# Attention scores: another order of sixteen key tiles, with one exponential over two neighbouring PSUM banks for ten of 32 score pairs

## The chip, the core and the metric

The kernel runs on one core of a Trainium2 chip. Its time is device microseconds of one execution. PE is the matrix engine (PEld is its weight loads), DVE the vector engine, ACT the scalar engine, POOL GpSimd, SP the engine that starts the DMAs.

## The reference, cut to what matters

Two layers, each an attention block and an MLP, on 2048 rows of 640 values in float32. The change touches attention alone:

```python
qkv = (x @ wqkv).reshape(B, S, 3, H, Dh)          # S 2048, H 32 heads, Dh 20
scores = einsum("bhqd,bhkd->bhqk", q, k) * Dh ** -0.5
p = softmax(scores, axis=-1)
o = einsum("bhqk,bhkd->bhqd", p, v)               # then @ wo, added to x
x = x + attention(layernorm(x)); x = x + mlp(layernorm(x))      # twice
```

## The kernel before

After the projections, attention runs in 32 blocks a layer. A block is four heads (a group g) and 512 queries (qb); it walks over sixteen tiles of 128 keys (kt). For each key tile there are four score matmuls (`score`, L713), one a head, each 128 keys by 512 queries into one PSUM bank; an exponential of each by ACT into an SBUF tile (L720), which is the softmax numerator because the row maximum is already subtracted through two extra rows of q and k; and the PV step (`pv`, L725), which adds exp times v of the four heads into bank 7. A 21st column of v gives the sum of the exponentials.

The four heads of a group are two pairs p, and of each pair one head (par 0) lies on PE's rows 0 to 63, the other (par 1) on rows 64 to 127, so that matmuls of different par run side by side.

The row maxima of a block have to be there before its scores. They are computed two blocks ahead, among the scores of the present block: a matmul with queries on the partitions (`by_queries`, L619) into a bank, and a maximum over it by DVE (L630). When all maxima of a block are there, `mrows_max` and `mrows` reduce and transpose them (two small DVE operations, L674 and L685), POOL splits them into two parts and a DMA writes them out; `mrows_load` brings them back two key tiles later as rows of q. This is called behind a PV step: at the first one at which the maxima are complete and the scores have begun key tile 4 of the block two ahead of the use (`state["begun"] >= (t - 2) * NKT + 4`). At the end of a block `finish` copies bank 7 (DVE, L738); its division follows in six steps in the next block, by POOL and DMAs.

What is issued when is written out by hand, in one string for the sixteen key tiles of a block (`ORDER_OF_BLOCK`, L1028), which `op` reads letter by letter (L1092): a and b are the next score of par 0 and of par 1 with its exponential, m and n the next maximum of par 0 and par 1, and V the next PV step. Each engine runs its instructions in the order in which they are issued. Four scores (abab) are issued ahead of the first block. When the maxima have run out, m and n do nothing. DMAs of q, k and v are started by `begin`, the first time that a score of a key tile is issued.

Seven banks (0 to 6) serve scores and maxima. Which one a row takes is decided while the kernel is built, by `Clock` (L505), a small model of PE, ACT and DVE in ns: it books each row's start, the exponential's or maximum's end and from that when each bank is free, and gives the bank that is free first. `value` books the PV step and the DVE operations that come with it: the copy at the last key tile, and 340 ns at key tile 4 for the two small ones. The model sets no order and adds no wait, it only chooses banks; semaphores keep the order between engines on the chip.

Of the kernel before, what the change touches and what calls it, by code (L numbers as in the profile page):

```python
# [10 lines left out]
AF = mybir.ActivationFunctionType  # L11
# [6 lines left out]
S = 2048  # L18
# [9 lines left out]
NKT = S // P  # L28
# [4 lines left out]
SCALE = DH ** -0.5  # L33
# [6 lines left out]
def tile_layers(  # L40
# [11 lines left out]
    nc = tc.nc  # L52
# [28 lines left out]
    banks = psum.tile([P, 8, 512], F32, tag="banks", name="banks")  # L81
# [424 lines left out]
    class Clock:  # L506
# [6 lines left out]
            self.act, self.act_end, self.dve = 0, 0, 0  # L513
            self.ready, self.used, self.acc = {}, [], 0

        def row(self, par):
            b = min(range(7), key=self.free.__getitem__)
            s = self.now + 3
            if self.values:
                s = self.now + 542  # L520
                self.values, self.fresh, self.place = False, [True, True], 0
                self.lane, self.over, self.since = [0, 0], [0, 0], None
            s = max(s, self.lane[par], self.load)
            w = max(s - 116, self.free[b] + 34)
            t = max(s, w + 61)
            more = max(0, w + 116 - t)
            if self.since is None:
                self.since = t
            self.now = t
            self.load = 0 if w + 177 < t else w + 116 + (46 if t > s + 10 else 0)  # L530
            self.lane[par] = t + 232 + more
            if self.fresh[par]:
                self.fresh[par] = False
                self.lane[par] = max(self.lane[par], self.since + 338)
            self.over[par] = t + more
            self.place += 1
            return b, t + more + {1: 532, 2: 563, 3: 465}.get(self.place, 433)

        def score(self, par, kt):
            b, t = self.row(par)  # L540
            if kt >= 3 and len(self.used) > kt - 3:
                t = max(t, self.used[kt - 3])
            t = max(t, self.act, self.act_end - 1958)
            self.act, self.act_end = t + 477, max(t + 592, self.act_end + 490)
            self.free[b] = self.act_end
            self.ready[kt] = self.act_end + 80
            return banks[:, b, :]

        def most(self, par):
            b, t = self.row(par)  # L550
            t = max(t, self.dve)
            self.dve, self.free[b] = t + 598, t + 641
            return banks[:, b, :]

        def value(self, kt):
            s = self.now + 453 if self.values else max(self.over) + 323
            s = max(s, self.ready.pop(kt), self.acc if kt % NKT == 0 else 0)
            self.load, self.values, self.now = 0, True, s + 453
            self.used.append(self.now + 747)
            if kt % NKT == NKT - 1:  # L560
                t = max(self.dve, self.now + 670)
                self.dve, self.acc = t + 598, t + 737
            if kt % NKT == 4:
                self.dve += 340
    QSEG = ((0, 0), (DH, 1), (2 * DH, 0))
    KSEG = ((0, 0), (DH, 0), (2 * DH, 1))

# [21 lines left out]
    def load_q(t):  # L589
        g, qb = divmod(t, NQB)  # L590
        q_t[t] = slot([P, 2, QB], F32R, "q")
        rows_of_heads(q_t[t], d_qk[0, :, :, qb * QB : (qb + 1) * QB], QSEG, g)
# [34 lines left out]
    def smax(dst, t, p, sub, c, par):  # L627

        by_queries(dst, t, p, sub, c, par)
        nc.vector.tensor_reduce(  # L630
            maxima(t)[:, 2 * p + par, sub, c : c + 1], dst, axis=AX.X, op=ALU.max
        )
# [72 lines left out]
    def score(dst, t, kt, h, es):  # L705

        p, par = divmod(h, 2)
        if p not in es:
            es[p] = weights[len(e_n) % len(weights)]
            e_n.append(t)  # L710
        b = 64 * par
        assert t in done
        nc.tensor.matmul(  # L713
            dst,
            k_t[t // NQB, kt // 4][b : b + 62, p, (kt % 4) * P : (kt % 4 + 1) * P],
            q_t[t][b : b + 62, p, :],
            start=True,
            stop=True,
        )
        nc.scalar.activation(es[p][:, par, :], dst, AF.Exp, scale=SCALE)  # L720

    def pv(acc, t, kt, es, heads=(3, 2, 1, 0)):
        for h in heads:
# [115 lines left out]
    def qkv(first, x_src, rest):  # L839
# [186 lines left out]


    ORDER_OF_BLOCK = (  # L1028
        "banmnabVanabmbaanVmnabmbVmbaanbbnmVbaananVbanmabVmbabanVmbmbbaVmnbmbaVab"
        "mbanmVannanabVbanmbaVanbmbaVbambmbVanmbanVmbabmnaV"  # L1030
    )

    def attention(first, x_src, first_rows):
        last = NBLK * NKT
        es_of = {}
        e_n.clear()
        weights.extend(slot([P, 2, QB], F32, "e") for _ in range(6))
        st_n, sm_n = [0, 0], [0, 0]
        state = {"begun": -1, "done": 0, "acc": None, "debt": 0}
        clock = Clock()  # L1040
# [20 lines left out]
        def begin(i):  # L1061

            t, u = divmod(i, NKT)
            g, qb = divmod(t, NQB)
            if u == 3:
                q_t.pop(t - 1, None)
            if u == 1:
                if t + 2 < NBLK and t + 2 not in q_t:
                    load_q(t + 2)
            if u % 4 == 1 and qb == 0:  # L1070
                k_t.pop((g - 1, u // 4), None)
                for h in (0, 1, 2, 3) if g else (1, 2):
                    if g + h < NG and (g + h, u // 4) not in k_t:
                        load_k(g + h, u // 4, True)
                if g and g + 3 >= NG:
                    del kept[(g - 1) % 4, u // 4]
            if u in (2, 10) and qb == NQB - 1 and g + 1 < NG:
                load_v(g + 1, u // 8)
            if first and t < 16 and u % 6 == 3:
                prep_job()  # L1080
            if first and t < 16 and u == 8:
                for sp in (w_o, w_1, w_2):
                    sp.save_full()
                    sp.past(sp.count, sp.got)
            if (t, u) in loads:
                loads[t, u]()
            if t == NBLK - 1 and u == 12:
                first_rows.extend(row_tile(x_src, i) for i in range(4))
            if i in split:
                split.pop(i)()  # L1090

        def op(o):  # L1092
            if o in "ab":
                par = "ab".index(o)
                i, p = divmod(st_n[par], 2)
                if i >= last:
                    return
                st_n[par] += 1
                if i > state["begun"]:
                    state["begun"] = i  # L1100
                    begin(i)
                dst = clock.score(par, i)
                score(dst, i // NKT, i % NKT, 2 * p + par, es_of.setdefault(i, {}))
            elif o in "mn":
                par = "mn".index(o)
                n = sm_n[par]
                if n == len(todo):
                    return
                t, p, sub, c = todo[n]
                if n == firsts[t] and par == 0:  # L1110
                    for s in blocks[blocks.index(t) :][:2]:
                        if s not in q_t:
                            load_q(s)
                if (t // NQB, c) not in k_t or t not in q_t:
                    return
                sm_n[par] += 1
                smax(clock.most(par), t, p, sub, c, par)
                if n == ends[t] and min(sm_n) > n:
                    over.add(t)
                    if t * NKT > state["begun"] + 2 * NKT:  # L1120
                        del q_t[t]
            else:
                i = state["done"]
                if i >= last or min(st_n) < 2 * (i + 1):
                    return
                t, u = divmod(i, NKT)
                if u == 0:
                    state["acc"] = banks[:, 7, :]
                clock.value(i)
                pv(state["acc"], t, u, es_of.pop(i))  # L1130
                state["done"] += 1
                if u == NKT - 1:
                    steps = finish(t, state["acc"])
                    split.update((i + j, f) for j, f in zip((4, 6, 7, 9, 11, 12), steps))
                t = rows["next"]
                if rows["at"] is not None:
                    if state["begun"] >= rows["at"]:
                        mrows_load(t)
                        rows.update(next=t + 1, at=None)
                elif t in over and t in q_t and state["begun"] >= (t - 2) * NKT + 4:  # L1140
                    mrows_max(t)
                    mrows(t)
                    rows["at"] = state["begun"] + 2

        for o in "abab":
            op(o)
        while state["done"] < last:
            for o in ORDER_OF_BLOCK:
                op(o)
# [228 lines left out]
```

## Time and profile before

| | |
|---|---|
| median of 3 runs | 3655.38 us (3650.18 to 3657.57) |
| profiled execution | 3654.16 us, its span 3652.4 us |
| granted TensorE clock, mean | 0.994 |
| busy share: PE, PEld | 98%, 59% |
| busy share: DVE, ACT, POOL | 73%, 74%, 24% |
| attention, first layer | about 359 to 1419 us of the span |
| attention, second layer | about 2175 to 3235 us of the span |

In the rows quoted below, a group's row has the line, the engine, the operation, output and input with their shapes and the count, then the busy time in us and the mean ns of one, then the engine's idle time ahead of them and what ended it. A row of the chain that ended last has the start in us, the length in us and the work; a row of the timeline has the same, with idle time and its releaser in brackets. The matmul groups show more records than the code has calls: one PV step is eight records of L725, two for each head.

### The profile page before, as it was taken

What the parts mean: (1) busy time and instruction counts of PE and PEld (TensorE: products, weight loads), DVE (VectorE), ACT (ScalarE), POOL (GpSimd) and SP (SyncE); (2) the same over time, 40 slices, a digit from 0 to 9 for tenths busy, and PEclk for the clock granted to TensorE, in tenths of its full rate; (3) what the DMA queues carried; (4) which work ended last, traced back from release to release, by engine and by line L of the source; (5) the groups of instructions that cost most, each with busy time, mean ns of one, the idle gap of its engine ahead of it and who ended that gap; (6) DMA issues with size and microseconds to landing.
All of it is one profiled execution on the core that took longest, in us unless ns stands there. A gap on an engine that the chain in (4) does not pass through costs nothing.

```text
span 3652.4 us, 70847 instructions
## 1 busy us (share of the span) xinstructions
PE 3593.7 (98%) x25492; PEld 2158.2 (59%) x25492; DVE 2649.2 (73%) x5208; ACT 2685.8 (74%) x5330; POOL 864.0 (24%) x993
## 2 busy tenths in 40 slices
PE   7999999999999999999999999999999999999999
PEld 5998333333333336989889973333333333368998
DVE  7998888888888881445469888888888888715543
ACT  2887999999999995122228879999999999942221
POOL 6540234322212211112163201212121112201210
PEclk9999999999999999999999999999999999999999
DMA  7665454432222135622357552222222121365221
GB/s 227 227 228 170 121 167 144 138 101 72 63 53 58 52 99 197 253 73 73 101 183 227 177 171 69 74 72 61 77 70 60 47 61 50 103 221 221 73 80 37
DMA packets 282799, 433.84 MB, mean 119 GB/s; under 512 B 71188, under 2 KB 130324, under 8 KB 282448
## 3 DMA queue, kind: packets, MB, share of 16 engines
q1 hardware_dynamic: 281904, 427.60, 37.7%
q8 instruction: 202, 3.31, 0.4%
q10 hardware_dynamic: 544, 1.71, 0.2%
q14 instruction: 149, 1.22, 0.1%
HBM read 284.48 MB, written 144.68 MB: 118 GB/s over the span
## 4 chain that ended last, share of the span: by engine, by line
PE 91%; DMA 3%; ACT 2%; DVE 2%; POOL 1%; issue 0%; SPq 0%; ACTq 0%; DVEq 0%; POOLq 0%
PE banks L725 27%; PE banks L336 20%; PE banks L713 17%; PE banks L619 17%; PE banks L365 5%; PE banks L356 4%; ACT e L720 2%; DMA k<-d_qk 1%; PE banks L451 0%; DVE x L252 0%; DVE bst L244 0%; DMA x<-d_x 0%; DVE h L257 0%; DVE r L1227 0%; ACT h L256 0%
## 5 line engine op out<-in xcount | busy, mean ns | idle before, releaser
L720 ACT ACTIVATE e<-banks 128x512 f32<-128x512 f32 x4096 | 2059.9, 641 | 77.3 <-PE banks L713 48.2
L630 DVE TENSOR_REDUCE mx<-banks 128x1 f32<-128x512 f32 x2560 | 1622.5, 684 | 377.2 <-PE banks L619 289.3
L725 PE MATMUL banks<-e,vg 128*32 128x512 f32 x8192 | 1096.7, 606 | 5.8 <-ACT e L720 5.2
L619 PE MATMUL banks<-k,q 60*128 60x512 f32 x3392 | 1058.0, 425 | 14.1 <-DMA q<-d_qk 12.0
L713 PE MATMUL banks<-q,k 62*128 62x512 f32 x4096 | 1035.2, 432 | 0.7 <-DVE mx L630 0.7
L713 PEld LDWEIGHTS banks<-q,k 62*128 62x128 f32 x4096 | 519.3, 185 | 613.7 <-ACT e L720 480.7
L619 PEld LDWEIGHTS banks<-k,q 60*128 60x128 f32 x3392 | 517.2, 185 | 381.2 <-ACT e L720 276.1
L659 DVE CUSTOM_DVE_ANT_0 rl<-banks,rl 128x512 f32<-128x512 f32 x704 | 456.4, 688 | 26.9 <-PE banks L619 7.0
L652 ACT ACTIVATE rl<-banks 128x512 f32<-128x512 f32 x704 | 382.1, 601 | 60.4 <-PE banks L619 43.1
L725 PEld LDWEIGHTS banks<-e,vg 128*32 128x32 f32 x8192 | 163.0, 108 | 347.8 <-issue 280.5
L336 PE MATMUL banks<-w,h 128*128 128x320 f32 x2304 | 349.4, 311 | 2.7 <-DVE h L257 2.5
L336 PEld LDWEIGHTS banks<-w,h 128*128 128x128 f32 x2304 | 339.3, 188 | 11.4 <-DVE h L257 6.4
L1226 ACT ACTIVATE r<-banks,b_t 128x512 f32<-128x512 f32 x96 | 66.1, 688 | 373.3 <-PE banks L336 227.3
L365 PE MATMUL banks<-xnT,wqk 64*128 64x512 f32 x1080 | 332.5, 397 | 1.6 <-DVE turned_t L358 1.6
L336 PE MATMUL banks<-xnT,w 128*128 128x512 f32 x1440 | 331.6, 391 | 0.0
L356 PE MATMUL banks<-xnT,wqk 64*128 64x512 f32 x1080 | 328.6, 396 | 0.0
L336 PEld LDWEIGHTS banks<-xnT,w 128*128 128x128 f32 x1440 | 270.8, 189 | 55.6
L769 POOL TENSOR_TENSOR few<-few,minus_t 128x16 f32<-128x16 f32 x62 | 179.8, 2901 | 256.9 <-DMA few<-d_s 248.5
L780 POOL TENSOR_TENSOR o<-o 128x512 f32<-128x512 f32 x62 | 79.6, 1283 | 572.2 <-DMA o<-d_r 316.6
L365 PEld LDWEIGHTS banks<-xnT,wqk 64*128 64x128 f32 x1080 | 203.0, 189 | 11.9 <-DVE turned_t L358 2.1
L619 PE MATMUL banks<-kd,q 60*128 60x512 f32 x704 | 207.8, 397 | 1.5 <-ACT rl L652 1.0
L356 PEld LDWEIGHTS banks<-xnT,wqk 64*128 64x128 f32 x1080 | 200.4, 188 | 11.5 <-issue 2.5
(88 smaller groups left out, 2728.0 us busy)
## 6 DMA issues: line engine op xcount, KB each, us to landing
q<-d_qk SPq DMA_DIRECT2D x888, 80.0 KB
d_qk<-ev SPq DMA_DIRECT2D x80, 512.0 KB
k<-d_qk SPq DMA_DIRECT2D x456, 80.0 KB
x<-d_x SPq DMA_DIRECT2D x96, 320.0 KB
d_o<-ot SPq DMA_DIRECT2D x248, 80.0 KB
ot<-d_o SPq DMA_DIRECT2D x38, 512.0 KB
d_v<-v SPq DMA_DIRECT2D x32, 512.0 KB
vg<-d_v SPq DMA_DIRECT2D x32, 512.0 KB
```

Of the source, the lines that this page charges most:

```text
L336: nc.tensor.matmul(dst, a, b, start=(n == 0), stop=(n == last))
L356: nc.tensor.matmul(dst, a[:64], b[:64], start=start, stop=last)
L365: nc.tensor.matmul(dst, a, b, start=False, stop=last, skip_group_check=True)
L619: nc.tensor.matmul(dst, q_t[t][b : b + 60, p, sub * P : (sub + 1) * P], k_t[t // NQB, c][b : b + 60, p, :], start=True, stop=True,)
L630: nc.vector.tensor_reduce(maxima(t)[:, 2 * p + par, sub, c : c + 1], dst, axis=AX.X, op=ALU.max)
L652: nc.scalar.activation(r, dst, AF.Relu)
L659: nc.vector.tensor_tensor_reduce(out=r[par], in0=dst, in1=r[par], scale=1.0, scalar=LEAST, op0=ALU.add, op1=ALU.max, accum_out=maxima(t)[: ...
L713: nc.tensor.matmul(dst, k_t[t // NQB, kt // 4][b : b + 62, p, (kt % 4) * P : (kt % 4 + 1) * P], q_t[t][b : b + 62, p, :], start=True, stop ...
L720: nc.scalar.activation(es[p][:, par, :], dst, AF.Exp, scale=SCALE)
L725: nc.tensor.matmul(acc[32 * h : 32 * h + 32, :], v_t[t // NQB, kt // 8][:, kt % 8, 32 * h : 32 * h + 32], es[p][:, par, :], start=(kt == 0 ...
L769: nc.gpsimd.tensor_tensor(few, few, minus_t, op=ALU.pow)
L780: nc.gpsimd.tensor_mul(o[:, 0, :], o[:, 0, :], o[:, 1, :])
```

## The change

1. `ORDER_OF_BLOCK` is another string. It has 44 single scores (22 a, 22 b), ten times the new letter S, the same 21 m, 21 n and 16 V.
2. S issues both scores of a pair (par 0 and par 1) into two neighbouring banks, and then one exponential over both, 1024 columns, into the whole SBUF tile of the pair. The exponential has moved out of `score` into `exps`; a and b still have one of 512 columns.
3. `Clock` has a step `both` for S: it takes the two neighbouring banks of 0 to 6 that are both free first, and frees both at the end of the wide exponential.
4. `Clock` books the release of a maximum's bank at 686 ns in place of 641, and the two small DVE operations as 448 ns at key tile 2 in place of 340 at key tile 4. When they are issued is decided as before, in `op`.

```diff
-        def row(self, par):
-            b = min(range(7), key=self.free.__getitem__)
+        def row(self, par, b):
...
-            return b, t + more + {1: 532, 2: 563, 3: 465}.get(self.place, 433)
+            return t + more + {1: 532, 2: 563, 3: 465}.get(self.place, 433)
+
+        def first(self):
+            return min(range(7), key=self.free.__getitem__)
 
         def score(self, par, kt):
-            b, t = self.row(par)
+            b = self.first()
+            t = self.row(par, b)
...
+        def both(self, kt):
+            b = min(range(6), key=lambda b: max(self.free[b : b + 2]))
+            t = max(self.row(par, b + par) for par in range(2))
+            if kt >= 3 and len(self.used) > kt - 3:
+                t = max(t, self.used[kt - 3])
+            t = max(t, self.act, self.act_end - 1958)
+            self.act, self.act_end = t + 897, max(t + 1015, self.act_end + 910)
+            self.free[b] = self.free[b + 1] = self.act_end
+            self.ready[kt] = self.act_end + 80
+            return banks[:, b : b + 2, :]
+
         def most(self, par):
-            b, t = self.row(par)
-            t = max(t, self.dve)
-            self.dve, self.free[b] = t + 598, t + 641
+            b = self.first()
+            t = max(self.row(par, b), self.dve)
+            self.dve, self.free[b] = t + 598, t + 686
             return banks[:, b, :]
...
-            if kt % NKT == 4:
-                self.dve += 340
+            if kt % NKT == 2:
+                self.dve += 448
...
-        nc.scalar.activation(es[p][:, par, :], dst, AF.Exp, scale=SCALE)
+
+    def exps(dst, src):
+
+        nc.scalar.activation(dst, src, AF.Exp, scale=SCALE)
...
     ORDER_OF_BLOCK = (
-        "banmnabVanabmbaanVmnabmbVmbaanbbnmVbaananVbanmabVmbabanVmbmbbaVmnbmbaVab"
-        "mbanmVannanabVbanmbaVanbmbaVbambmbVanmbanVmbabmnaV"
+        "bbannaVbamnabmVnabmnabVSnanbmVnambabmVSbmnaVSnabmVSnSmVbmamnSVbmanbanVan"
+        "abmbmVbambannVbmabanmVSmbanVSnabmVSnSmVm"
     )
...
-            if o in "ab":
-                par = "ab".index(o)
-                i, p = divmod(st_n[par], 2)
+            if o in "abS":
+                pars = (0, 1) if o == "S" else ("ab".index(o),)
+                i, p = divmod(st_n[pars[0]], 2)
+                assert len(pars) == 1 or st_n[0] == st_n[1]
...
+                es = es_of.setdefault(i, {})
+                dst = clock.both(i) if o == "S" else clock.score(pars[0], i)
+                for par in pars:
+                    st_n[par] += 1
+                    score(
+                        dst[:, par, :] if o == "S" else dst,
+                        i // NKT, i % NKT, 2 * p + par, es,
+                    )
+                exps(es[p] if o == "S" else es[p][:, pars[0], :], dst)
```

More of the change, by code (lines that the diff above doesn't have):

```diff
@@ L1092, in op @@
         def op(o):
-            if o in "ab":
-                par = "ab".index(o)
-                i, p = divmod(st_n[par], 2)
+            if o in "abS":
+                pars = (0, 1) if o == "S" else ("ab".index(o),)
+                i, p = divmod(st_n[pars[0]], 2)
+                assert len(pars) == 1 or st_n[0] == st_n[1]
                 if i >= last:
                     return
-                st_n[par] += 1
                 if i > state["begun"]:
@@ L1101, in op @@
                     begin(i)
-                dst = clock.score(par, i)
-                score(dst, i // NKT, i % NKT, 2 * p + par, es_of.setdefault(i, {}))
+                es = es_of.setdefault(i, {})
[7 more added lines that the diff above has]
+                exps(es[p] if o == "S" else es[p][:, pars[0], :], dst)
             elif o in "mn":
```

## The prediction

> **What bounds the kernel now.** I read the page first (span, busy shares, the chain by engine, the costliest groups), then a table of stretches, then one block of the chain that ended last.
>
> ```profile
> span 3652.4 us, 70847 instructions
> PE 91%; DMA 3%; ACT 2%; DVE 2%; POOL 1%; issue 0%; SPq 0%; ACTq 0%; DVEq 0%; POOLq 0%
> L720 ACT ACTIVATE e<-banks 128x512 f32<-128x512 f32 x4096 | 2059.9, 641 | 77.3 <-PE banks L713 48.2
> L630 DVE TENSOR_REDUCE mx<-banks 128x1 f32<-128x512 f32 x2560 | 1622.5, 684 | 377.2 <-PE banks L619 289.3
> ```
>
> PE carries 91% of the chain. The change touches attention alone: 2 layers of 32 blocks, 64 exponentials (L720) in each. The maxima (L630) come 42 to a block, so 2560 of them last 2560 / 42 = 61 blocks; in the other 1.5 blocks of each layer there are none.
>
> The table of stretches has the first layer's 30 whole blocks in one row, and what follows in the next (bounds, length, then PE, PEld, DVE, ACT, POOL).
>
> ```profile
> 359.20:1355.70 996.50, 996.50 (x7013) 381.25 (x7005) 818.82 (x1344) 964.21 (x1916) 260.63 (x280) 1.00 0.34 97
> 1355.70:1418.60 62.90, 59.99 (x404) 19.82 (x400) 14.96 (x25) 61.96 (x126) 12.57 (x10) 1.00 0.49 149
> ```
>
> 996.5 / 30 = 33.22 us a block, with PE busy throughout at full clock, ACT 97% and DVE 82%. Two engines are near their limit, so the average settles nothing. The chain of one block does: each row is the eight PV matmuls (L725) that end a key tile, and the distance from row to row is one **stretch** of score and maximum rows and its PV.
>
> ```profile
> 992.21 1.00 PE banks L725 x8
> 994.96 0.99 PE banks L725 x8
> 996.86 1.00 PE banks L725 x8
> 999.87 1.00 PE banks L725 x8
> 1001.77 1.00 PE banks L725 x8
> ...
> 1009.36 1.00 PE banks L725 x8
> 1011.48 0.99 PE banks L725 x8
> 1013.61 0.99 PE banks L725 x8
> ...
> 1021.20 1.00 PE banks L725 x8
> 1023.32 0.99 PE banks L725 x8
> 1025.45 0.55 PE banks L725 x2
> ```
>
> Set the order string beside it. The a and m rows use one half of PE's rows, the b and n rows the other, and the halves run side by side; so what counts in a stretch is its fuller half. Per block ten stretches have 3 rows in it, four have 4, two have 5. Measured: 3 rows 1.90 us (four stretches from 1001.77 to 1009.36, 7.59 / 4 = 1.90), 4 rows 2.12 and 2.13 (1009.36 to 1011.48 to 1013.61), 5 rows **2.75** (992.21 to 994.96) and **3.01** (996.86 to 999.87). The fourth row costs 0.23; the fifth costs 0.62 and 0.88. Both five-row stretches hold nine rows, and there are seven banks for them: the eighth row needs a bank that a row of the same stretch has just filled. The timeline shows a row of the second one waiting for that:
>
> ```profile
> 998.23 0.21 DVE L674 TENSOR_REDUCE nm<-mx 128x16 f32<-128x64 f32 x1
> 998.54 0.21 DVE L685 STREAM_TRANSPOSE nt<-nm 128x32 f32<-128x32 f32 x1
> 998.67 2.44 DVE L630 TENSOR_REDUCE mx<-banks 128x1 f32<-128x512 f32 x4
> ...
> 999.38 0.18 PEld L619 LDWEIGHTS banks<-k,q 60*128 60x128 f32 x1 [0.19 <-DVE mx L630]
> ```
>
> The other part of the 3.01 is the pair in the first two rows: DVE is away from the banks for 0.52 us (998.23 to 998.75). In a later block that pair ran elsewhere, inside the first five-row stretch, and its price went with it:
>
> ```profile
> 1323.90 1.00 PE banks L725 x8
> 1326.96 0.99 PE banks L725 x8
> 1328.86 1.00 PE banks L725 x8
> 1331.56 1.00 PE banks L725 x8
> ```
>
> ```profile
> 1323.52 0.21 DVE L674 TENSOR_REDUCE nm<-mx 128x16 f32<-128x64 f32 x1
> ```
>
> There the first takes 3.06 and the second 2.70. So the pair costs 3.06 - 2.75 = 3.01 - 2.70 = 0.31 us.
>
> **The change, part by part.** *The order.* Counting the new string in the same way, no stretch has five rows: six have 3, ten have 4, and none holds more than seven rows, as many as there are banks. By the measured lengths a block is 6 x 1.90 + 10 x 2.13 = 32.7. The old one by the same lengths is 10 x 1.90 + 4 x 2.13 + 2.75 + 3.01 = 33.3 (33.22 measured; rounding adds 0.06). With 1.897 for 1.90 and 2.127 for 2.13 it is 33.24 against 32.65: **-0.59 us** a block. No PE row, no maximum and no DMA is added or removed; loads are called as a key tile begins, and the order of tiles is the same, so SP's queue is passed by nothing.
>
> *The pair of small DVE operations* isn't removed. It is issued behind the PV at which the scores have reached key tile 4. In the new string that is the fourth PV, with twelve maxima since the block's copy in place of nine, while the planner books it at key tile 2 (448 ns). So the banks are planned for an idler DVE than there will be. The next stretch has three maxima in 2.13 us:
>
> ```profile
> 1323.97 3.72 DVE L630 TENSOR_REDUCE mx<-banks 128x1 f32<-128x512 f32 x6
> ```
>
> Those run one every (3.72 - 0.68) / 5 = 0.61, so 1.83 + 0.52 = 2.35 in 2.13: DVE comes out 0.22 late, and what follows is a pair of scores (S) that needs two neighbouring banks at once. Bounds: 0 if other banks are free, 0.52 if all of DVE's absence reaches PE. Nearest measured: 0.31. I take 0.26, between 0.22 and 0.31: **+0.26**, behind the fourth or fifth PV.
>
> *One exponential for two.* No instruction over 1024 columns is in this trace, so its length is bounded. ACT alone, back to back, is seen where the maxima have run out (timeline, then the groups); the price of a column comes from two copies of different width.
>
> ```profile
> 1356.45 61.51 ACT L720 ACTIVATE e<-banks 128x512 f32<-128x512 f32 x124
> ```
>
> ```profile
> L420 ACT COPY v<-banks 128x320 f32<-128x320 f32 x64 | 27.5, 430 | 11.1 <-PE banks L713 4.9 <-DMA k<-d_qk 1.6 <-issue 1.6
> L263 ACT COPY r<-banks 128x512 f32<-128x512 f32 x88 | 51.7, 590 | 111.4 <-PE banks L451 56.9 <-PE banks L365 21.6 <-DVE mx L644 20.9
> ```
>
> A single exponential holds ACT (61.51 - 0.64) / 123 = 0.495; a column costs (590 - 430) / 192 = 0.833 ns. A wide one is then 0.495 + 512 x 0.833 ns = **0.92**, between 0.85 (columns alone) and 0.99 (two singles). ACT's work in a block falls from 64 x 0.495 = 31.7 to 44 x 0.495 + 10 x 0.92 = 31.0. ACT is off the path in most stretches, so I book no gain. What it does is keep the new order alive: the three-row stretches now stand three together, and each brings four exponentials, as S and two singles (1.91) or two S (1.84), against a stretch of 1.90. At 0.92 ACT keeps step; four singles (1.98) would not. Against it, a wide one gives its first bank back only when both are read, 0.43 later than a single would; with at most seven rows in a stretch I book nothing more for this than the 0.26.
>
> The Trainium skill, "ScalarE: Activation LUTs", section "What ACT_TABLE_LOAD costs", gives an activation with immediate operands 186 ns + 0.833 ns a column, of which back-to-back ones overlap 93. The slope agrees with the two copies; the fixed part does not: it would make a single 0.52 where the trace has 0.495, and a wide one 0.946 (an estimate from that page; no run here shows one yet).
>
> *Where no maxima are left* (1.5 blocks a layer) ACT is the bound: 61.96 of 62.90 us above. Ten wide ones save 10 x 0.07 = 0.7 a block there, at most 2.1 for both layers; PV waits and short stretches may eat it. I take -1.0, bounds 0 and -2.1.
>
> **Sum.** 61 x (-0.59 + 0.26) - 1.0 = **-21 us**. The profiled execution took 3654.2 (span 3652.4), 1.2 below the median of 3655.4, so 3633 by it and **3634** as a median.
>
> **The rivals.**
>
> *The pair finds free banks* (the 0.26 is 0). For: the stretch after it has 0.23 more than a three-row one, and a late maximum delays PE only if it holds the very bank asked for. Against: in both places where it stands now it costs 0.31. Then 61 x -0.59 - 2 = -38: 3617.
>
> *A somewhat longer wide exponential.* From about 0.935 on, ACT falls behind within a triple of three-row stretches, whose first two ask 1.91 of 1.90 already, and the PV behind them waits for its exponentials. At 0.945 ten of them cost 0.25 a block, less some 0.1 that the stretch between an exponential and its PV absorbs: -0.33 + 0.15 = -0.18, or 61 x -0.18 - 0.5 = -11.5: 3644. By the skill page's 0.946 this rival is the case.
>
> *Slower: the wide one costs what two singles cost.* Place: the last PVs of the two triples. Each wide one is then 0.07 dearer, ACT needs 31.7 again, in an order that leaves it no five-row pauses to catch up. 10 x 0.07 = 0.7 a block, less 0.15 absorbed: -0.33 + 0.55 = +0.22, so 61 x 0.22 = +13: 3668. It decides from (0.33 + 0.15) / 10 = 0.048 above 0.92, about 0.97. For: a PSUM read across a bank border is nowhere in the trace. Against: the slope of the copies, at which a border would have to cost 50 ns.
>
> *The waits only move.* If ACT's idle 1.5 us a block (33.22 - 31.7) is forced by the PVs and grows by as much as its work shrinks, the block stays at 33.2 and the change doesn't do what the order says: 3655. Against: nothing ties it to 33.2, since 31.0 + 1.5 = 32.5 is under the 32.65 that PE needs.
>
> **How the numbers follow.** Forecast (3624 to 3640) 0.55; free banks (3615 to 3624) 0.17; longer wide one (3640 to 3651) 0.14; waits move (3651 to 3660) 0.05; slower (3660 to 3680) 0.09. The range 3616 to 3652 holds all of the first and third and most of the second. A measurement of this kernel tells about 0.2% (7 us) from no change. Faster by more, under 3648: 0.55 + 0.17 + two thirds of 0.14 = 0.81; slower, over 3662.7: 0.09; the rest, 0.10, is within it.
>
> **What would show it.** In the chain of a block after: stretches of 1.90 and 2.13 alone, with one of about 2.15 (three rows) or 2.4 behind the fourth or fifth PV, and a row there released by DVE's maximum. A block of 32.9. Wide exponentials about 0.43 longer than singles in the groups. Wrong would be: PV weight loads released by ACT in the triples (the wide one is dearer), more than one stretch off its length, or a block at 32.65 (the pair was free).

## The result and the profile after

The median went from 3652.99 us to **3630.05** (3625.21 to 3632.64, four runs of each); the ratio is 0.9934, 95% interval 0.9917 to 0.9952. That is 22.9 us or 0.6% less. The forecast of 3634 started from 3655.38, the median of three of the four runs of the kernel before; 2.4 of the 4 us between forecast and result are this.

The profiled execution took 3625.21, its span:

```profile
span 3623.4 us, 70898 instructions
```

One block of the chain, as the kernel is now (start, length, work). The line numbers have moved: L742 is the PV, L727 the score, L633 the matmul of a maximum, L644 the maximum, L737 the exponential (with two singles and with the small operation the same, with the pair doubled three lines further on from L727; the kernel before keeps its own).

```profile
1013.55 1.00 PE banks L742 x8
1015.68 0.99 PE banks L742 x8
...
1022.05 0.99 PE banks L742 x8
1024.13 0.99 PE banks L742 x8
1026.04 1.00 PE banks L742 x8
1027.94 0.99 PE banks L742 x8
1030.08 0.99 PE banks L742 x8
...
1044.24 0.99 PE banks L742 x8
1046.39 1.00 PE banks L742 x8
```

Sixteen stretches lie between the first row and the last, 32.84 us against 33.24 before. Over the 2nd to the 30th block of a layer the mean is 32.88 against 33.22. None has five rows. Four-row stretches take 2.13 (1013.55 to 1015.68), three-row ones 1.91 and 1.90 (1024.13 to 1027.94). Two kinds stand off their length: the three-row stretch from 1022.05 takes **2.08**, and the four-row ones behind a triple of three-row stretches take 2.14 and 2.15 (from 1027.94 and from 1044.24).

The groups of ACT, by form, show the two exponentials:

```profile
L737 ACT ACTIVATE e<-banks 128x512 f32<-128x512 f32 x2824 | 1478.4, 608 | 45.4 <-PE banks L727 15.6 <-PE banks L633 10.3
L737 ACT ACTIVATE e<-banks 128x1024 f32<-128x1024 f32 x636 | 642.9, 1035 | 20.7 <-PE banks L727 5.4
```

A wide one lasts 427 ns longer than a single: 512 columns at 0.834 ns. The border between the banks costs nothing that can be seen. Where one wide exponential directly follows another, their ends lie 0.92 us apart.

By the PV records, the first layer's attention goes from 1060.06 us (358.41 to 1418.48) to 1048.80 (354.23 to 1403.04), the second's from 1060.28 to 1048.74: together 22.8 us, which is the difference of the medians. The two profiled executions differ by 28.9; the other 6 lie ahead of the first PV and between the layers, almost all of it in code that the change leaves alone. The stage between the layers by itself took between 751.7 and 759.7 in the kernels below.

### The profile page after: what moved, and what is told of

Same layout as the page of the kernel before. It is cut to its first block, busy times and chain, and to the rows that moved or that the text cites. A ratio compares the mean times of both kernels' runs of the same rounds, so it can differ in the third digit from the quotient of the medians.

```text
span 3623.4 us, 70898 instructions
## 1 busy us (share of the span) xinstructions
PE 3569.3 (99%) x25492; PEld 2164.7 (60%) x25492; DVE 2647.8 (73%) x5208; ACT 2672.7 (74%) x4694; POOL 865.6 (24%) x993
## 4 chain that ended last, share of the span: by engine, by line
PE 91%; DMA 3%; DVE 2%; ACT 2%; issue 1%; POOL 0%; SPq 0%; ACTq 0%; DVEq 0%; POOLq 0%
PE banks L742 27%; PE banks L336 21%; PE banks L727 17%; PE banks L633 16%; PE banks L365 5%; PE banks L356 4%; DMA k<-d_qk 1%; ACT e L737 1%; DMA q<-d_qk 1%; PE banks L451 0%; SPq L76 0%; DVE h L257 0%; DVE r L1251 0%; PE banks L351 0%; DMA raw<-in_A_wqkv_dram 0%
## 5 line engine op out<-in xcount | busy, mean ns | idle before, releaser
L737 ACT ACTIVATE e<-banks 128x512 f32<-128x512 f32 (+1 forms) x3460 | 2046.3, 687 | 66.0 <-PE banks L727 21.0
L644 DVE TENSOR_REDUCE mx<-banks 128x1 f32<-128x512 f32 x2560 | 1618.5, 684 | 354.5 <-PE banks L633 280.4
L742 PE MATMUL banks<-e,vg 128*32 128x512 f32 x8192 | 1098.2, 605 | 6.1 <-ACT e L737 5.4
L633 PE MATMUL banks<-k,q 60*128 60x512 f32 x3392 | 1085.6, 411 | 12.8 <-DMA q<-d_qk 11.6
L727 PE MATMUL banks<-q,k 62*128 62x512 f32 x4096 | 1056.1, 443 | 0.0
L727 PEld LDWEIGHTS banks<-q,k 62*128 62x128 f32 x4096 | 517.6, 185 | 746.0 <-ACT e L737 466.7
L633 PEld LDWEIGHTS banks<-k,q 60*128 60x128 f32 x3392 | 580.2, 185 | 209.4 <-ACT e L737 63.7
L742 PEld LDWEIGHTS banks<-e,vg 128*32 128x32 f32 x8192 | 163.9, 108 | 358.1 <-issue 278.2
L633 PE MATMUL banks<-kd,q 60*128 60x512 f32 x704 | 206.1, 398 | 0.6 <-DMA kd<-d_kd 0.4
```

The costliest lines, as they stand in the source:

```text
L633: nc.tensor.matmul(dst, q_t[t][b : b + 60, p, sub * P : (sub + 1) * P], k_t[t // NQB, c][b : b + 60, p, :], start=True, stop=True,)
L644: nc.vector.tensor_reduce(maxima(t)[:, 2 * p + par, sub, c : c + 1], dst, axis=AX.X, op=ALU.max)
L727: nc.tensor.matmul(dst, k_t[t // NQB, kt // 4][b : b + 62, p, (kt % 4) * P : (kt % 4 + 1) * P], q_t[t][b : b + 62, p, :], start=True, stop ...
L737: nc.scalar.activation(dst, src, AF.Exp, scale=SCALE)
L742: nc.tensor.matmul(acc[32 * h : 32 * h + 32, :], v_t[t // NQB, kt // 8][:, kt % 8, 32 * h : 32 * h + 32], es[p][:, par, :], start=(kt == 0 ...
```

## The experiments

Three theories. **Order**: time goes where a stretch has more rows than banks, so the new order gains, wide exponentials only let ACT keep its pace, and the pair of small DVE operations takes back 0.2 to 0.3 a block. **Wide**: the gain is ACT's saved time. **Planner**: the gain is the choice of banks.

### The new order with two singles for each wide one

```diff
-                exps(es[p] if o == "S" else es[p][:, pars[0], :], dst)
+                for par in pars:
+                    exps(es[p][:, par, :], dst[:, par, :] if o == "S" else dst)
```

> The changed kernel, but S issues two exponentials of 512 columns for its two neighbouring banks; order and banks are the same. Theory 'order' (the gain comes from stretches without a fifth row; wide exponentials only let ACT keep up in the triples of three-row stretches): ACT needs 10 x 0.07 = 0.7 us more a block, the PV at the end of each triple comes 0.1 to 0.2 late, the block goes from 32.88 to about 33.15, the time to about 3647, still a little under before. Theory 'wide' (the gain is ACT's 0.7 a block): all of it is lost, the block is back at 33.24 or above, 3653 or more. Theory 'planner' (the banks chosen are the gain): 3630, no change.

Measured: 3649.83, ratio to before 0.9996 (0.9987 to 1.0004). The chain, around the triples:

```profile
1021.67 0.99 PE banks L742 x8
...
1036.05 1.00 PE banks L742 x8
1038.34 1.00 PE banks L742 x8
...
1052.56 0.99 PE banks L742 x8
1054.86 1.00 PE banks L742 x8
```

The block is 33.19 (1021.67 to 1054.86); the two stretches behind the triples take 2.29 and 2.30 where the changed kernel has 2.14 and 2.15, and that is the whole difference but 0.05. Over the 2nd to the 30th block the mean is 33.19, 0.31 above the changed kernel. So the order without wide exponentials gains nothing. That is near what theory "order" gave (33.15), but theory "wide" is not excluded by it.

### Wide exponentials in the old order

Six where the string allows them, then five at other places. Only the string differs from the changed kernel:

```diff
-        "bbannaVbamnabmVnabmnabVSnanbmVnambabmVSbmnaVSnabmVSnSmVbmamnSVbmanbanVan"
-        "abmbmVbambannVbmabanmVSmbanVSnabmVSnSmVm"
+        "SnmnSVanabmbaanVmnabmbVmbaanbbnmVSananVbanmabVmbabanVmbmbSVmnbmbaVab"      # six
+        "mbanmVannanabVbanmbaVanbmbaVbambmbVanmSnVmSbmnaV"
+        "SnmnSVanabmbaanVmnabmbVmbaanbbnmVSananVbanmabVmbabanVmbmbbaVmnbmbaVab"     # five
+        "mbanmVannanabVbanmbaVanbmbaVbmSmbVanmbanVmbamnSV"
```

> The old order of the tiles with wide exponentials alone: the six places where its string has a score of each half side by side and both counts are equal become S; planner as in the changed kernel. Theory 'order': both five-row stretches stay, so the block is not under 33.2, and since S now asks for two neighbouring banks in them it may be longer, up to 34: 3653 to 3700. Theory 'wide': ACT saves 6 x 0.07 = 0.42 a block, 61 x 0.42 = 26 us, so about 3628.

Measured: 3733.24, ratio 1.0229 (1.0215 to 1.0242), *slower*. The timeline shows the stretch that lost most:

```profile
1084.00 1.06 PE L742 MATMUL banks<-e,vg 128*32 128x512 f32 x8
...
1085.80 1.88 DVE L644 TENSOR_REDUCE mx<-banks 128x1 f32<-128x512 f32 x3
...
1086.54 0.18 PEld L727 LDWEIGHTS banks<-q,k 62*128 62x128 f32 x1 [1.01 <-DVE mx L644]
...
1086.96 0.16 PEld L742 LDWEIGHTS banks<-e,vg 128*32 128x32 f32 x8 [0.24 <-issue]
```

The weight load of one score of the S sits idle 1.01 us until a maximum has left its bank, and the one exponential over both halves waits with it. A four-row stretch takes 2.96 (1084.00 to 1086.96) where others take 2.13: this one S, whose two banks are not free together, costs 0.83, more than ten of them save (0.7).

> The old order with five wide exponentials at places where two neighbouring banks should be free (two of them need a score moved past one or two letters of its stretch; the rows of each stretch and the PVs stay). Theory 'order': the two five-row stretches decide, ACT's saved time is not on the path, block 33.2, 3651 within 5 us. Theory 'wide': ACT saves 5 x 0.066 = 0.33 a block, 20 us, about 3631.

Measured: 3650.67, ratio 0.9997 (0.9988 to 1.0006). Both five-row stretches are as they were:

```profile
1024.05 0.99 PE banks L742 x8
1025.95 0.99 PE banks L742 x8
1028.96 0.99 PE banks L742 x8
...
1054.57 0.99 PE banks L742 x8
1057.31 0.99 PE banks L742 x8
```

They take 3.01 (from 1025.95) and 2.74 (from 1054.57), and the block 33.26 (1024.05 to 1057.31). ACT has 0.33 less to do in each block, and nothing comes of it there. With that theory "wide" falls: saved ACT time alone, at these five places, is worth nothing in the old order. The end of a layer, where no maxima are left, is the exception; it comes to 0.7 us in all and is taken up below.

### The old order with the new planner's numbers

The changed kernel with the old string, so without S.

> The old order with the changed planner's numbers (686, 448 at key tile 2), no wide exponential: only banks can differ from before. Theories 'order' and 'wide': block 33.2, 3653 within 5 us. Theory 'planner': about 3630.

Measured: 3651.85, ratio 1.0003 (0.9994 to 1.0012). Theory "planner" falls: the new numbers alone bring nothing in the old order. The new order with the old numbers was not run, so what the new numbers add to it stays open.

### A small operation behind each wide exponential

```diff
                 exps(es[p] if o == "S" else es[p][:, pars[0], :], dst)
+                if o == "S":
+                    nc.scalar.copy(table_t, eps_t)
```

> The changed kernel, with a copy of 128 x 1 on ACT behind each wide exponential, so that the two together hold ACT about as long as two singles (0.915 + 0.06 = 0.98). Banks are given back when they were. If what two singles cost is ACT's time in the triples: the eighth and the sixteenth stretch grow from 2.14 to 2.3, the block to 33.2, the time to about 3648, as with two singles. If it was that there were two instructions with their waits: 3630.

Measured: 3648.12, ratio 0.9990 (0.9981 to 0.9998), as with two singles. In the stretch behind the first triple the timeline names what waits, in the changed kernel and in this one:

```profile
1029.57 0.19 PEld L727 LDWEIGHTS banks<-q,k 62*128 62x128 f32 x2 [0.17 <-ACT e L737]
```

```profile
1035.03 0.21 ACT L1129 COPY table_t<-eps_t 128x1 f32<-128x1 f32 x1
1035.11 1.06 ACT L737 ACTIVATE e<-banks 128x1024 f32<-128x1024 f32 x1
...
1036.22 0.19 PEld L727 LDWEIGHTS banks<-q,k 62*128 62x128 f32 x2 [0.30 <-ACT e L737]
```

The copy puts the next exponential 0.08 later (1035.03 to 1035.11), and the last rows of the stretch wait 0.30 for a bank in place of 0.17. The stretch grows by as much, from 2.14 (1027.87 to 1030.01 in this view) to 2.27 (1034.38 to 1036.65). So it is ACT's time in the triples, and it reaches PE through a bank that is given back late.

### The pair of small DVE operations: moved, doubled, and moved in the kernel before

```diff
-                elif t in over and t in q_t and state["begun"] >= (t - 2) * NKT + 4:
+                elif t in over and t in q_t and state["begun"] >= (t - 2) * NKT + 6:
```

> The changed kernel, with the two small DVE operations issued when the scores have reached key tile 6, not 4, so behind the PV after the next but one stretch, where two maxima a stretch leave DVE idle. The maxima are the same, and the rows come back two key tiles later, more than a block ahead of their use. If the pair makes the 2.07 stretch (1.90 without, 0.175 a block), that goes: block 32.70, 61 x 0.175 = 10.7 us less, about 3619. If the stretch is long for another reason (the wide exponential, the pair of banks): no change, 3630.

Measured: **3620.05**, ratio to before 0.9916 (0.9902 to 0.9930), the fastest kernel here. The stretch that took 2.08 is at its length:

```profile
1012.14 0.99 PE banks L742 x8
...
1020.68 0.99 PE banks L742 x8
1022.58 1.00 PE banks L742 x8
...
1044.88 0.99 PE banks L742 x8
```

1.90 from 1020.68, and a block of 32.74 (1012.14 to 1044.88).

Doubled in place, with the reduce and the transpose each in a loop of two:

> The changed kernel, with each of the two small DVE operations (reduce of the maxima, transpose) issued twice at its place, 0.4 to 0.5 us more of DVE a block. If the pair delays PE through the banks, its stretch grows by as much, from 2.08 to about 2.5, and the block to 33.3: 61 x 0.43 = 26 us more, about 3656. If DVE has room there (the 2.08 has another cause): 3630 to 3635.

Measured: 3654.75, ratio 1.0008 (0.9999 to 1.0017).

```profile
1033.12 0.46 DVE L702 STREAM_TRANSPOSE nt<-nm 128x32 f32<-128x32 f32 x2
1033.26 0.16 PEld L745 LDWEIGHTS banks<-e,vg 128*32 128x32 f32 x8 [0.37 <-issue]
...
1033.50 1.85 DVE L644 TENSOR_REDUCE mx<-banks 128x1 f32<-128x512 f32 x3
...
1034.80 0.18 PEld L730 LDWEIGHTS banks<-q,k 62*128 62x128 f32 x1 [0.37 <-DVE mx L644]
...
1035.83 0.16 PEld L745 LDWEIGHTS banks<-e,vg 128*32 128x32 f32 x8 [0.24 <-issue]
```

The second half of the S waits for a maximum that DVE began late, and the three-row stretch takes 2.57 (1033.26 to 1035.83). The second pair costs 0.49 in this stretch, about its whole length: beyond the first, nothing is left to hide it.

The same line edited in the kernel before, and nothing else:

> The kernel before, with one number changed: the two small DVE operations are issued when the scores have reached key tile 6, not 4, behind a three-row stretch with idle DVE. Neither the order nor the exponentials change. If the pair is worth the 0.31 by which 3.01 stands above 2.70: block 32.92, 61 x 0.31 = 19 us, about 3632, as much as the whole change. If the fourth stretch of before is long because of its nine rows alone: 3651.

Measured: 3635.75, ratio 0.9951 (0.9938 to 0.9963).

```profile
1017.29 0.99 PE banks L725 x8
1019.18 0.99 PE banks L725 x8
1021.89 0.99 PE banks L725 x8
...
1050.21 1.00 PE banks L725 x8
```

The nine-row stretch takes 2.71 (1019.18 to 1021.89) in place of 3.01, and the block 32.92 (1017.29 to 1050.21). Against the runs of the kernel before that were taken with it (3651.82), one number in the old kernel brings 16 us, where the whole change brings 23.

The timeline of this stretch also shows what is left to gain in it:

```profile
1021.33 0.24 PEld L619 LDWEIGHTS banks<-k,q 60*128 60x128 f32 x2 [0.35 <-ACT e L720]
```

Its last two rows wait 0.35 for a bank that an exponential gives back, and 1.90 + 2 x 0.23 + 0.35 is the 2.71. So a fifth row costs what a fourth does, and a wait for a bank. That this comes of nine rows over seven banks fits these figures; no run here has another number of banks.

Set this kernel against the one with the new order and the pair moved. With the pair out of the way in both, the mean block is 32.93 in the old order and 32.73 in the new. So of the 0.34 that the change brings in a block, 0.20 is the order with its wide exponentials. The other 0.14 is the pair, which costs 0.29 in the old order and 0.15 in the new.

## Why the prediction was right, point by point

- **The lengths of the stretches** held: 1.90 and 2.13, none of five rows, and a block of 32.84, on average 32.88, where 32.9 was forecast. The old order with singles or with five wide ones, and with the old or the new banks, stayed at 33.2; with six wide ones it grew to 34.7.
- **The pair** was priced at +0.26 and measured +0.18 (2.08 against 1.90). The mechanism was right: it goes when the pair is moved, and it grows when the pair is doubled. The size was 0.08 too high, 5 us in all, and by whole blocks (32.88 against 32.73) it was 0.11 too high. In the changed kernel itself the trace names no maximum as the releaser in that stretch; only the doubled pair shows it by name.
- **Luck in the block.** Without the pair the new block was to take 32.65; with the pair out of the way it took 32.73, and two of the stretches that are too long are those behind the triples. So the order was priced 0.08 too well and the pair 0.11 too dear. The two misses nearly cancel, which nothing in the prediction foresaw, and the forecast gain of 0.33 came out at 0.34.
- **The wide exponential** was put at 0.92, with no gain booked but the pace of ACT. Its 427 ns over a single confirm the slope, and the 0.92 between the ends of two of them the sum; the two runs in which a wide one is made about as dear as two singles lose 18 to 20 us, nearly all of the gain. The place was another than the rival gave: not the PV at the end of a triple waits, but the last rows of the stretch behind it, for a bank. The PV weight load at the end of a triple is put down to ACT in the changed kernel (idle 0.38 at 1027.87), which was named as a sign of a dearer wide one; but its stretch keeps to 1.90, so nothing is lost by it. Nor was the price right: two singles cost 0.31 to 0.35 a block and not 0.55, so even then the kernel would have been level with before, not 13 us slower.
- **Where no maxima are left**, -1.0 was booked. From the start of the 31st block to the last PV a layer takes 60.94 in place of 61.43: -1.0 for both layers. That this is ACT's time is borne out by the others: 61.08 with five wide ones in the old order, 61.43 in the old order with the new numbers, 61.9 in the new order with two singles.
- **Left out** was the first block of each layer: 0.84 and 1.03 shorter where an ordinary block gains 0.34, so 1.2 more in all. It is not shown to belong to the change. The same block varies without it: 35.41 and 35.28 in the kernel before, 34.07 and 34.76 there with the pair moved, 34.75 and 34.30 in the old order with the new numbers, and 35.16 and 35.29 in the new order with two singles. What makes it vary stays open.
- The sum was -21 and came out at -22.9; less the 1.2 of the first blocks, attention became 21.6 shorter. The rival "free banks" (3617) would have been right with the pair two key tiles later, which ran at 3620. With the estimate of 0.946 from the Trainium skill, "ScalarE: Activation LUTs", section "What ACT_TABLE_LOAD costs", the time would have been 3644. The measurement decides against it: 0.92 from end to end, and 3630.

## What to carry to other kernels

Where several engines share a ring of banks, count the rows between two fixed points and set them against the banks: with at most seven rows for seven banks a row more cost 0.23 us here, and with nine it cost 0.6, of which some 0.35 was the wait for a bank. Look at what an engine has to do besides its rows at just that point: moving 0.4 us of small operations by two key tiles was worth 16 us in the old order and 10 in the new, against 23 for the whole change. A wide exponential saved its fixed part, 0.07 us, only where both its banks were free together; where they weren't, it cost the wait for the later one.

## What was not expected of the hardware

The wide read passes from one PSUM bank to the next with no visible cost (0.834 ns a column, as within a bank). And the price of asking for two neighbouring banks can be far above the 0.07 us that a wide exponential saves: 0.83 us in the stretch of one S in the old order.
